# Four interleaved attention layers on one core: larger matmul pieces in crowded chunks, even pacing in the others, and another order at a layer's end

## The chip, the cores and the metric

The kernel runs on one core of one Trainium2 chip. The metric is the device time of one launch in microseconds (us); the median of three runs is used. Engines: TensorE (PE) does matmuls, ScalarE (ACT) the exponentials, VectorE (DVE) and GpSimd (POOL) the elementwise work, SyncE (SP) issues the DMAs.

## The reference

The input x has 2048 rows (positions) of 512 features. Four layers follow each other: A, B, A, B. Each adds an attention block to its input; A and B have their own weights, and both layers of a kind use the same ones.

```python
# H = 32 heads, Dh = 16, S = 2048, D = 512
qkv = layernorm(x) @ wqkv          # split into q, k, v, 32 heads of 16
scores = q @ k.T * 16 ** -0.5
# A: only 0 <= i - j < 256 is kept (a sliding window); B: all of it
p = softmax(scores)
x = x + (p @ v) @ wo
```

## The kernel before

Layers are numbered 0 to 3: 0 and 2 are the sliding ones (A), 1 and 3 the dense ones (B). Queries are taken in four chunks `c` of 512 columns. A chunk has eight groups `qd` of four heads. In a sliding layer a group has three steps (`WTILES`), so a chunk has 24 steps. In each step TensorE makes two score tiles (L722), ScalarE takes their exponential (L726), GpSimd zeroes what lies outside the window (L789, L792: five or so selects of 128x256 a step), and TensorE multiplies with the values (`PV`, L799). The PV of a step is issued two steps later (`pvq`, `flush(2)`). After a group's last PV an epilogue on VectorE (L694 to L710) divides by the sums and makes two fp16 halves of the output, `oh`.

Everything else is *side work*, laid between the steps: projections of keys `K(l, c)` and queries `Q(l, c)`, values `VV(l, c)`, the output projection with residual, statistics and normalisation `OO(l, c)`, DMA transposes of the normalised rows `T(l, c)`, preparation of weights `PR`. For layer 3, keys and queries come in quarters of the heads: `K3(c, ht)`, `Q3(c, ht)`. A projection consists of units: each unit accumulates 12 matmuls into one of two PSUM banks (an fp16 product in three terms over four blocks of 128) and is then evicted by ScalarE and VectorE. `VV` with half of the heads has matmuls 256 wide instead of 512. The names in the profile: `w`, `w_h` weights of keys and queries, `wv` of values, `wo` of the output, `xc` the transposed input, `sp` the evicted projection, `sq` its squares.

Python writes the order of TensorE's instructions once, when the kernel is built; the chip runs them in that order. A model clock (`clock`, 0.222 us a matmul) decides what is ready. In each step of a sliding layer, `Side.step` first issues transposes and preparation that are due, then side work until the amount spent reaches `due`, which grows linearly to the chunk's whole cost at step 22; at most about 3 us a step. A unit is cut into pieces of `RUN = 4` matmuls. `finish()` issues at the chunk's end what is left, with no step in between. Weights are loaded when a work is opened, and two can be open at a time (`WB = 2`). A `T` becomes due 9 us of the model clock after its `OO`, its four transposes 2.3 us apart, and is counted as done 6 us after the last.

`keys` and `queries` end with squares: a matmul (L557) of each unit's squares sums them per head; for keys VectorE takes the maximum (L573), for queries it writes a row `m` (L585, L589) that a DMA stores beside the queries. `key_shift` (L599) takes the maximum over the chunks and writes a row `mk` beside the keys `kf`; the dense layer's loads `kt<-kf` read it. Before, `mk` and `m` shared one buffer (tag `m`).

Costs that decide below: `PK = 48 * MM + 0.3` = 10.96 for K or Q, `PV = PO` = 10.66 for VV or OO, a quarter for K3, half for a VV of half the heads.

## Time and profile before

| | us |
|---|---|
| median of 3 runs | 2760.53 (2757.52 to 2761.16) |
| the profiled execution, its own time | 2759.46 |
| its span, first to last instruction | 2757.7 |
| PE busy | 2633.6 (95%) |
| ACT busy | 2385.2 (86%) |
| DVE busy | 955.0 (35%) |
| POOL busy | 566.3 (21%) |

A stage is read from its own rows, not from the shares of the whole: the dense layers run from about 509 to 1463 us and from 1787 us on, the sliding layers before each of them. In a timeline row stand the start, the duration, engine, source line, operation, output and inputs, the number of instructions merged, and in brackets how long the engine was idle before and what ended that. A row of a table by stretches has the stretch, its length, and each engine's busy time with the number of instructions, then the granted clock of TensorE, the DMA engines' share and GB/s. A row of waits has who waited for whom, the total in us, how often, and the longest.

### The profile page before, as it was taken

What the parts mean: (1) busy time and instruction counts of PE and PEld (TensorE: products, weight loads), DVE (VectorE), ACT (ScalarE), POOL (GpSimd) and SP (SyncE); (2) the same over time, 40 slices, a digit from 0 to 9 for tenths busy, and PEclk for the clock granted to TensorE, in tenths of its full rate; (3) what the DMA queues carried; (4) which work ended last, traced back from release to release, by engine and by line L of the source; (5) the groups of instructions that cost most, each with busy time, mean ns of one, the idle gap of its engine ahead of it and who ended that gap; (6) DMA issues with size and microseconds to landing.
All of it is one profiled execution on the core that took longest, in us unless ns stands there. A gap on an engine that the chain in (4) does not pass through costs nothing.

```text
span 2757.7 us, 59654 instructions
## 1 busy us (share of the span) xinstructions
PE 2633.6 (95%) x24358; PEld 776.5 (28%) x24358; DVE 955.0 (35%) x2059; ACT 2385.2 (86%) x2687; POOL 566.3 (21%) x1129
## 2 busy tenths in 40 slices
PE   8988999999999999999999989899999999999997
PEld 4333344322222222222223333522222222222221
DVE  7668756111131113211315676412222222222222
ACT  3665665799999999999996778399999999999997
POOL 2576663000000000000004688100000000000000
PEclk9999999999999999999999999999999999999999
DMA  6876766422232224222325474623334343333331
GB/s 217 230 222 209 220 212 191 141 78 72 94 92 89 71 86 111 78 68 81 109 72 161 152 202 135 179 63 103 110 112 122 120 120 105 102 110 114 98 95 56
DMA packets 317501, 344.78 MB, mean 125 GB/s; under 512 B 113056, under 2 KB 233376, under 8 KB 311200
## 3 DMA queue, kind: packets, MB, share of 16 engines
q1 hardware_dynamic: 317216, 340.86, 40.8%
q8 instruction: 193, 3.16, 0.5%
q14 instruction: 92, 0.75, 0.1%
HBM read 228.07 MB, written 96.99 MB: 118 GB/s over the span
## 4 chain that ended last, share of the span: by engine, by line
PE 74%; DVE 7%; ACT 7%; issue 6%; DMA 3%; POOL 2%; SPq 0%; ACTq 0%; DVEq 0%; POOLq 0%
PE acc L766 30%; PE s L722 19%; PE acc L434 10%; PE b L437 9%; ACT e L726 6%; PE acc L799 4%; PE bs L437 1%; DVE ot L694 1%; DVE xh L476 1%; DVE sp L535 1%; DVE xh L470 1%; DVE xn L470 1%; DMA kt<-kw 1%; POOL e L789 0%; DMA xc<-xh 0%
## 5 line engine op out<-in xcount | busy, mean ns | idle before, releaser
L726 ACT ACTIVATE e<-s 128x1024 f32<-128x1024 f32 (+2 forms) x2432 | 2244.8, 1122 | 135.0 <-PE s L722 121.7
L766 PE MATMUL acc<-e,vt 128*17 128x512 f32 x8192 | 1077.9, 598 | 5.4 <-DVE ot L694 4.5
L722 PE MATMUL s<-qt,kt 64*128 64x512 f16 (+3 forms) x5504 | 774.9, 355 | 58.6 <-ACT e L726 32.3
L722 PEld LDWEIGHTS <-kt 64*128 64x128 f16 x5504 | 202.6, 94 | 807.9 <-issue 779.3
L792 POOL TENSOR_SCALAR_AFFINE_SELECT e<-e 128x256 f32<-128x256 f32 x512 | 226.6, 450 | 118.0 <-ACT e L726 117.6
L766 PEld LDWEIGHTS acc<-e,vt 128*17 128x17 f32 x8192 | 136.2, 95 | 379.7 <-issue 347.8
L694 DVE STREAM_TRANSPOSE ot<-acc 128x512 f32<-128x512 f32 x128 | 91.4, 714 | 400.6 <-PE acc L766 317.5
L710 POOL TENSOR_TENSOR oh<-o,oh 128x512 f16<-128x512 f32 x31 | 36.0, 1161 | 885.9 <-DVE oh L709 885.9
L789 POOL TENSOR_SCALAR_AFFINE_SELECT e<-e 128x256 f32<-128x256 f32 x448 | 199.1, 451 | 69.6 <-ACT e L726 67.8
L799 PE MATMUL acc<-e,vt 128*17 128x384 f32 (+2 forms) x2816 | 199.9, 394 | 1.9 <-POOL e L789 1.0
L437 PE MATMUL b<-xc,w 128*128 128x512 f16 x672 | 164.8, 392 | 10.8 <-DVE sp L535 8.3
L540 POOL TENSOR_TENSOR sq_h<-sp_h 128x512 bf16<-128x512 f16 x27 | 28.1, 1040 | 488.5 <-DVE sp_h L534 488.5
L534 DVE TENSOR_SCALAR sp<-acc,es 128x512 f16<-128x512 f32 x28 | 20.9, 748 | 288.9 <-PE acc L434 277.2
L534 DVE TENSOR_SCALAR sp_h<-acc,es 128x512 f16<-128x512 f32 x27 | 20.3, 751 | 286.5 <-PE acc L434 277.8
L434 PE MATMUL acc<-xc,w_h 128*32 128x512 f16 x1296 | 108.6, 379 | 2.3 <-DVE km L573 2.3
L540 POOL TENSOR_TENSOR sq<-sp 128x512 bf16<-128x512 f16 x28 | 29.1, 1040 | 397.2 <-DVE sp L534 397.2
L434 PE MATMUL acc<-xc,w 128*32 128x512 f16 x1344 | 108.9, 379 | 0.3
L646 DVE COPY vt<-acc 128x256 f32<-128x256 f32 (+1 forms) x36 | 18.5, 513 | 258.2 <-PE acc L434 258.2
L681 DVE TENSOR_TENSOR dx<-acc,gcol 128x512 f32<-128x512 f32 x60 | 41.5, 692 | 176.8 <-PE acc L434 176.8
L434 PE MATMUL acc<-wo,oh 128*32 128x512 f16 x1296 | 101.3, 379 | 0.0
L437 PEld LDWEIGHTS <-w 128*128 128x128 f16 x720 | 67.0, 100 | 114.8 <-issue 49.3
L437 PE MATMUL b<-wo,oh 128*128 128x512 f16 x390 | 95.1, 384 | 2.3 <-DVE dx L660 2.1
(167 smaller groups left out, 1754.3 us busy)
## 6 DMA issues: line engine op xcount, KB each, us to landing
kt<-kf SPq DMA_DIRECT2D x128, 512.0 KB
qt<-qs SPq DMA_DIRECT2D x128, 256.0 KB
xd<-x SPq DMA_DIRECT2D x96, 256.0 KB
x<-xd SPq DMA_DIRECT2D x96, 256.0 KB
w<-wd SPq DMA_DIRECT2D x20, 1024.0 KB
kt<-kw SPq DMA_DIRECT2D x64, 256.0 KB
qs<-sp SPq DMA_DIRECT2D x48, 256.0 KB
wo<-wd SPq DMA_DIRECT2D x12, 1024.0 KB
```

The costliest lines, as they stand in the source:

```text
L434: nc.tensor.matmul(ps[g:g + 32], a[:, g:g + 32], b, start=(i == 0), stop=(i == len(pairs) - 1), skip_group_check=True)
L437: nc.tensor.matmul(ps, a, b, start=(i == 0), stop=(i == len(pairs) - 1))
L470: norm1 = lambda o: nc.vector.tensor_scalar(o, xs[i], mv[:, i, 0:1], y[:, i:i + 1], op0=ALU.subtract, op1=ALU.mult)
L540: nc.gpsimd.tensor_tensor(sq, sp[:, 0], sp[:, 0], ALU.mult)
L681: nc.vector.tensor_tensor(d, ps, gcol[1], ALU.mult)
L694: nc.vector.transpose(ot.rearrange("p b r -> p (b r)"), a)
L722: nc.tensor.matmul(ps[:, h, s0:s0 + wd_], kt[R * h:R * h + R, pr, kc:kc + P], qt[R * h:R * h + R, pr, qc:qc + wd_], start=True, stop=True)
L726: nc.scalar.activation(e[:, :, w0:w1], ps[:, :, w0:w1], AF.Exp, scale=SCALE)
L766: nc.tensor.matmul(a[32 * h:32 * h + DH + 1, :], V[l, qd // 4, j // 8][:, j % 8, 4 * (qd % 4) + h, :], es_[h // 2][:, h % 2, :], start=(j ...
L789: nc.gpsimd.affine_select(v, v, pattern=[[0, 2], [-1, P]], compare_op=ALU.is_gt, fill=0.0, base=0, channel_multiplier=1)
L792: nc.gpsimd.affine_select(v, v, pattern=[[0, 2], [1, P]], compare_op=ALU.is_ge, fill=0.0, base=0, channel_multiplier=-1)
L799: nc.tensor.matmul(a[32 * h:32 * h + DH + 1, q * P:(q + nb) * P], V[l, (4 * c + j) // 4][:, j % 4, 4 * qd + h, :], es_[h // 2][:, h % 2, s ...
```

## The change

1. A chunk of a sliding layer whose side work costs less than `FEW * MM * steps` = 7 x 0.222 x 24 = 37.3 us keeps pieces of four; the others issue whole units of 12. In chunks with pieces of four, `due` is no longer cumulative: each step takes an equal part of what is left over the steps left, less half a piece.
2. In layer 2, `VV(3, 0)` for the first half of the heads moves from the tail after the last chunk into that chunk, and `K3(2, 0)` moves from the chunk to the head of the tail.
3. After layers 0 and 2 the key shift, which first issues the waiting squares, becomes a work that is ready 1.2 us of the model clock later, so that a unit of the last values may come before it.
4. The shift's row has a buffer of its own, 128 wide instead of 512, and is stored in 16 pieces a head instead of 4.

```diff
-RUN = 4
+RUN, FEW = 4, 7
...
-        PH["unit"], PH["now"], PH["extra"] = None, None, 0
+        PH["unit"], PH["now"], PH["extra"], PH["run"] = None, None, 0, 12
...
-                elif PH["win"] and i % RUN == RUN - 1:
-                    yield RUN * us
+                elif i % PH["run"] == PH["run"] - 1:
+                    yield PH["run"] * us
...
-        m = vp.tile([P, QC], F16, name=f"mk{l}_{ht}", tag="m", bufs=1)
-        nc.vector.tensor_scalar(m[r], ones[r], kx[r], -0.515, op0=ALU.mult, op1=ALU.mult)
+        m = vp.tile([P, P], F16, name=f"mk{l}_{ht}", tag="mk", bufs=1)
+        nc.vector.tensor_scalar(m[r], ones[r, :P], kx[r], -0.515, op0=ALU.mult, op1=ALU.mult)
         for t in range(NHT) if ht is None else (ht,):
-            nc.sync.dma_start(rows(kf)[8 * t:8 * t + 8, 7, :].rearrange("h (c n) -> h c n", n=QC),
-                              m[32 * t:32 * t + 8, None, :].broadcast_to([8, NQ, QC]))
+            nc.sync.dma_start(rows(kf)[8 * t:8 * t + 8, 7, :].rearrange("h (c n) -> h c n", n=P),
+                              m[32 * t:32 * t + 8, None, :].broadcast_to([8, NT, P]))
...
             s0, due = self.spent, self.cost * self.k / (self.steps - 2)
+            if PH["run"] < 12:
+                due = s0 + (self.cost - s0) / max(self.steps - self.k, 2) - RUN / 2 * MM
             while self.q and self.spent < due and self.spent - s0 < 3:
...
+                if win:
+                    PH["run"] = RUN if sd.cost < FEW * MM * sd.steps else 12
                 ops = load(l, c, qds[0])
...
+    def shifted(l, ht):
+        key_shift(l, ht)
+        yield -1e-6
...
-        return [OO(2, 2), T(3, 2), K3(2, 0, True)]
+        return [OO(2, 2), VV(3, 0, True, (0,)), T(3, 2)]
...
-             2: [VV(3, 0, True, (0,)), OO(2, 3, True), VV(3, 1, True, (0,), late(3)), VV(3, 2, True, (0,), late(3)), Q3(0, 0, True, late(3)), T(3, 3), K3(3, 0, True)]}
+             2: [K3(2, 0, True), OO(2, 3, True), VV(3, 1, True, (0,), late(3)), VV(3, 2, True, (0,), late(3)), Q3(0, 0, True, late(3)), T(3, 3), K3(3, 0, True)]}
...
-            key_shift(l + 1, 0 if l else None)
-            all_of(lasts[l], works[l + 1][0])
+            shift = Work(later(lambda: shifted(l + 1, 0 if l else None)), 0.0)
+            shift.ready = clock[0] + 1.2
+            all_of([shift] + lasts[l], works[l + 1][0])
```

The remaining hunks replace `RUN if PH["win"] else 12` by `PH["run"]` where a unit ends, and let `shift3` call `shifted`.

More of the change, by code (lines that the diff above doesn't have):

```diff
@@ L549, in project @@
                 nc.sync.dma_start(d[:, 2], sp[:, 0])
-            yield -MM if PH["full"] else -(RUN if PH["win"] else 12) * MM
+            yield -MM if PH["full"] else -PH["run"] * MM
         return sqs
@@ L646, in values @@
                     nc.vector.tensor_copy(to, fr)
-            yield -us if PH["full"] else -(RUN if PH["win"] else 12) * us
+            yield -us if PH["full"] else -PH["run"] * us
     def wo(l, c, tail):
@@ L665, in wo @@
                 XN[l + 1, c] = norm(l + 1, c, xs, tail)
-            yield -MM if PH["full"] else -(RUN if PH["win"] else 12) * MM
+            yield -MM if PH["full"] else -PH["run"] * MM
     def wo_part(c, t):
@@ L1022, in Q3 @@
         return Work(later(queries, 3, c, act, ht), PK / 4, ("Q3", c, ht), [("T", 3, c), *after], True)
+    def shifted(l, ht):
+        key_shift(l, ht)
+        yield -1e-6
     def shift3(ht):
-        def gen():
-            key_shift(3, ht)
-            yield -1e-6
-        return Work(gen(), 0.0, None, [("K3", c, ht) for c in range(NQ)])
+        return Work(shifted(3, ht), 0.0, None, [("K3", c, ht) for c in range(NQ)])
     def O3(c, ht):
```

## The prediction

> **What bounds the kernel now.** I read the page first, then a table of the stages, then who waits for whom in the sliding layers, then TensorE's timeline at the places the change touches.
>
> ```profile
> span 2757.7 us, 59654 instructions
> ...
> PE   8988999999999999999999989899999999999997
> ```
>
> The two dense layers fill most of the span and nothing in them is edited but one buffer. TensorE's row falls below 9 in slices 1 to 8 and 20 to 26 of 69 us: the two sliding layers. I cut these into their chunks of 512 queries:
>
> ```profile
> core 0: us, PE busy (x) PEld busy (x) DVE busy (x) ACT busy (x) POOL busy (x), PEclk, DMA share, GB/s
> 65.30:142.80 77.50, 68.62 (x521) 23.72 (x521) 50.01 (x110) 47.95 (x71) 42.12 (x95) 0.93 0.83 231
> 142.80:243.10 100.30, 88.50 (x780) 35.35 (x779) 70.12 (x144) 63.28 (x78) 71.28 (x150) 0.97 0.72 221
> 243.10:357.60 114.50, 102.53 (x845) 41.21 (x844) 83.25 (x161) 70.68 (x89) 77.24 (x140) 0.94 0.75 213
> 357.60:450.90 93.30, 90.18 (x859) 39.09 (x858) 54.35 (x115) 63.19 (x78) 61.17 (x149) 1.00 0.70 216
> ...
> 1462.90:1534.30 71.40, 64.90 (x516) 22.90 (x513) 45.73 (x107) 44.51 (x64) 38.46 (x92) 0.95 0.63 199
> 1534.30:1603.70 69.40, 63.06 (x684) 24.48 (x680) 48.75 (x109) 52.36 (x58) 56.56 (x134) 1.00 0.57 165
> 1603.70:1669.60 65.90, 63.19 (x686) 24.88 (x686) 45.07 (x102) 49.55 (x55) 53.22 (x125) 1.00 0.65 183
> 1669.60:1724.00 54.40, 50.11 (x609) 19.71 (x608) 36.56 (x83) 44.28 (x48) 48.04 (x119) 1.00 0.39 118
> 1724.00:1743.80 19.80, 13.06 (x108) 7.43 (x109) 12.56 (x29) 4.16 (x7) 6.62 (x15) 0.83 0.65 153
> 1743.80:1786.80 43.00, 38.15 (x269) 25.72 (x267) 19.88 (x44) 11.48 (x25) 0.00 (x0) 1.00 0.69 193
> ```
>
> Four chunks of layer 0, four of layer 2, then layer 2's end in two rows. TensorE is the busiest engine in every row, so its instructions, which the change only reorders, are a floor; what can be won or lost is its idle time. The worst row is 1724.0 to 1743.8: 13.06 of 19.80 us busy, at 0.83 of the clock.
>
> In layer 0's four chunks TensorE waits for these, in us:
>
> ```profile
> PE s L722 <- ACT e L726: 17.5, 21, 3.6
> PE b L437 <- DVE sp L535: 8.3, 6, 3.2
> ...
> PE b L437 <- DVE dx L660: 2.1, 1, 2.1
> ```
>
> The first is scores held up because ScalarE has not emptied a score buffer; the other two are projection units held up because a bank is not yet evicted.
>
> The price of a step with and without side work, from the last chunk of layer 2:
>
> ```profile
> 1692.23 0.61 PE L722 MATMUL s<-qt,kt 64*128 64x128 f16 x8
> ...
> 1694.74 0.39 PE L722 MATMUL s<-qt,kt 64*128 64x256 f16 x4 [0.52 <-ACT e L726]
> ...
> 1697.02 0.61 PE L722 MATMUL s<-qt,kt 64*128 64x384 f16 x8
> ...
> 1698.55 1.04 PE L437 MATMUL b<-wo,oh 128*128 128x512 f16 x4
> 1699.52 0.61 PE L722 MATMUL s<-qt,kt 64*128 64x128 f16 x8
> ```
>
> A step with one piece of four runs from 1697.02 to 1699.52, 2.50 us. The bare step at 1692.23 and the step with a piece after it take 4.79 together, so an isolated bare step costs 2.29. A piece adds about 0.97, so TensorE alone would need 2.50 - 0.97 = 1.53 for a bare step: about 0.7 us is lost at each. In a row of bare steps ScalarE sets the pace: 44.28 us for 48 exponentials is 0.92 each, 1.85 a step.
>
> **Layer 2's end.** This is the largest term.
>
> ```profile
> 1724.59 2.05 PE L799 MATMUL acc<-e,vt 128*17 128x128 f32 x16 [0.60 <-DVE ot L694]
> 1732.67 4.11 PE L437 MATMUL b<-xc,w_h 128*128 128x512 f16 x12 [6.03 <-DMA xc<-xh]
> 1736.71 1.92 PE L799 MATMUL acc<-e,vt 128*17 128x256 f32 x32
> 1738.56 1.48 PE L437 MATMUL b<-wv,xc 128*128 128x256 f16 x12
> ...
> 1743.81 0.38 PE L437 MATMUL b<-wo,oh 128*128 128x512 f16 x1
> ```
>
> The key unit of chunk 2, K3(2,0), stands in order ahead of the last two PV groups and waits 6.03 us for its transposed input; the last PVs, their epilogue and the whole tail wait behind it. Then four half-width value units fill the time until O is ready, and the output projection begins at 1743.81. What releases it:
>
> ```profile
> 1711.96 0.68 DVE L660 TENSOR_TENSOR dx<-b,gcol 128x512 f32<-128x512 f32 x1
> ...
> 1730.22 0.40 POOL L792 TENSOR_SCALAR_AFFINE_SELECT e<-e 128x256 f32<-128x256 f32 x1
> ...
> 1738.70 0.72 DVE L694 STREAM_TRANSPOSE ot<-acc 128x512 f32<-128x512 f32 x1 [0.41 <-PE acc L799]
> ...
> 1741.80 0.69 DVE L710 TENSOR_TENSOR oh<-o,oh 128x512 f16<-128x512 f32 x1
> ```
>
> The epilogue after the last PV takes 1742.49 - 1738.63 = 3.9 us. GpSimd's last select ends at 1730.62, so the last PV could not have begun before that.
>
> The change puts the value units VV(3,0) into the chunk and K3(2,0) at the head of the tail. The chunk's cost becomes 10.66 + 5.33 = 15.98; by the new formula every step owes at least 15.98/24 - 0.44 > 0, so a piece is issued in each step from the fourth on: 12 output pieces in steps 4 to 15, then the 12 half-wide value pieces. The stage starts at 1669.6, three bare steps at 1.9 bring it to 1675.3, and 12 x 2.50 to 1705.3; OO(2,2) then ends some 6 us before the 1712.0 that the dx row marks, and the normalisation and its transposes (landed at 1732.67, 20.7 us after that dx) come at about 1726. The value pieces cost 1.48/3 = 0.49 a step in steps that otherwise wait for ScalarE (1.53 + 0.49 = 2.02 against 1.85): nearly nothing, and 9 steps at 2.1 to 2.2 end the scores at about 1724, as before. GpSimd has some 33 selects left at step 19 (begun about 1712) at 0.40 (48.04/119) to 0.5 us: last select 1727 to 1730; PVs done at about 1730 (1728 to 1731). K3(2,0) runs inside the 3.9 us of the epilogue. The output projection starts at about 1734 (1732 to 1737) instead of 1743.8: **-9.5 us (-7 to -12)**. The late end is K3(2,0) still waiting for its transposes. The cover that is lost, the value units, was worth 5.2 us; the epilogue is now bare for 3.9 - 2.76 = 1.1 us.
>
> On the clock: the unit behind the 6.03 us gap took 4.11 us where the same unit takes 2.76 at 1598.79 (row below). The Trainium skill, "TensorE: Matmul & The Clock Gate", Part 1, says that an idle window of about 3.4 us halves the clock; the trace agrees for this gap. By that rule the new waits, shorter and split by K3(2,0), may leave the clock whole; I take nothing for it either way.
>
> **The other chunks of layer 2, new pacing.** In pieces of four, a step now takes the rest of the cost over the rest of the steps instead of catching up.
> - Chunk 0 (cost 32.6): before, its last unit work came in blocks of 16 and left the last three steps bare. Spread out, it saves two or three bare steps at 0.7: -2 us (-4 to 0).
> - Chunk 1 (24.4): the formula gives one piece a step for 15 steps. Two units of queries come first (6 pieces, as OO(2,0) is not loaded yet), so OO(2,0) ends in step 17 instead of 14, 44 us into the stage instead of 39.
>
> ```profile
> 1572.55 1.04 PE L437 MATMUL b<-wo,oh 128*128 128x512 f16 x4
> ...
> 1598.79 2.76 PE L437 MATMUL b<-xc,w_h 128*128 128x512 f16 x12
> ...
> 1603.71 0.61 PE L722 MATMUL s<-qt,kt 64*128 64x128 f16 x8 [2.16 <-DMA kt<-kw]
> ```
>
> K3(0,0) ran 25.2 us after OO's last piece without a wait; by the 20.7 us above its input has 4 us to spare, which the 5 us use up. SyncE's queue is in order, so the loads of the next chunk stand behind these transposes too (the 2.16 us). Against it, the bare steps before K3 shrink. +1.5 us (-2 to +6).
> - Chunk 2 (24.1): OO(2,1) ends in step 13, some 6 us later, but value units and two bare steps still separate it from K3(1,0): -0.5 us (-3 to +3).
>
> **Layer 0.** Chunk 0 (35.6, under the limit of 7 x 0.222 x 24 = 37.3) gets the even pacing: no blocks of 12 that outrun the eviction, fewer bare steps at the end: -2 us (-5 to +3). Chunks 1 to 3 (47.7, 54.2, 48.9) go to whole units of 2.664 at 2.17, 2.46 and 2.22 a step, so some 4, 2 and 4 steps get none: 10 x 0.7 = +7. Against that, one unit a step gives each bank a full step to be evicted: of 8.3 + 2.1 us of bank waits I take half, -5; and fewer breaks (three pieces 3 x 0.97 against 2.70 for a unit in place, 0.2 each, about ten): -2. Sum 0 (-7 to +7). The longest bank wait, 3.2 us, I leave, because the eviction stands in VectorE's queue behind a normalisation.
>
> **The squares and the shift's buffer.**
>
> ```profile
> 497.63 0.38 PE L557 MATMUL bs<-sq,hsum 128*32 128x512 bf16 x1 [0.86 <-ACT sq L538]
> ...
> 509.14 0.61 PE L722 MATMUL s<-qt,kt 64*128 64x512 f16 x4 [0.67 <-DMA kt<-kf]
> ```
> ```profile
> 1775.72 0.38 PE L557 MATMUL b<-sq_h,hsum 128*32 128x512 bf16 x1 [1.12 <-ACT sq_h L538]
> ...
> 1779.04 0.34 DVE L606 TENSOR_SCALAR mk<-ones,kx 32x512 f16<-32x512 f16 x1 [2.05 <-DMA qs<-m]
> ...
> 1782.10 1.63 SPq L743 DMA_DIRECT2D kt<-kf  x3
> ...
> 1786.81 0.73 PE L722 MATMUL s<-qt,kt 64*128 64x512 f16 x4
> ```
>
> After layer 0 the dense layer waits for its keys, which wait for the shift, which waits for the last square at 497.63; filling TensorE before it moves idle time behind it: 0 (-1 to +1.5). After layer 2 both ends move: TensorE's work ends 1.1 us earlier, and the shift no longer waits 2.05 us for the queries' row: -1 us (-1.2 to +1.6). The shift's row is now written in pieces of 256 bytes. The Trainium skill, "DMA: Bandwidth & Descriptors", Specifications, says that writes under 512 bytes cost a read-modify-write; no run here shows it. Taking that transfer at twice the time between its issue and the keys' issue, an estimate by that page, the -1 would be about +1.6.
>
> **Sum.** -9.5 - 2 + 1.5 - 0.5 - 2 + 0 + 0 - 1 = -13.5 us. The profiled execution took 2759.46 us, so 2746; the median of the runs, 2760.53, is 1.1 above it: **2747 us**.
>
> **Rivals.**
> - *The banks were the price in layer 0.* All bank waits (10.4) vanish rather than half, and the ones of ScalarE shrink with even chunks: 10 us more, 2737. For it: 3.2 us is one wait. Against: VectorE is 0.70 to 0.73 busy there and in order.
> - *The refill only moves the wait.* K3(2,0) still waits in the tail, or VectorE's normalisation under the last selects holds GpSimd and the PVs. Then the end gives 3 to 4 us and the sum is -7: 2753, and with chunk 1 at its bad end 2758.
> - *The pacing starves the keys.* OO late in chunks 1 and 2, K3 put in order before its input has landed, in both, each with the half clock that the 4.11 us row shows: +5 + 1.4 and +6 + 1.4 more, and the 7 us of bare steps in layer 0 with nothing back: 2747 + 21 = 2768. It decides if OO(2,0) ends more than 4 us later. Against: bare steps before K3 absorb most of it.
>
> **Chances.** Forecast 0.58; banks 0.14; moved wait 0.17; starved keys 0.11. The wait of 6.03 us in front of the last PVs is the surest item. What lies under 2755 (0.2%, about what a measurement of this kernel can tell from no change) is the forecast, the banks and a little of the moved wait: faster 0.74; same 0.15; slower 0.11. The independent bounds add, root of squares, to about 8 us; reaching towards the moved wait gives 2737 to 2759.
>
> **What would show it.** Right: at layer 2's end no wait of TensorE over 4 us and OO within 10.5 us of the last score; scores of that chunk still ending near 54 us after its start; clock over 0.9 there. Chunk 0 of layer 2 without blocks of 16. Wrong: a w_h unit waiting for xc in any chunk; layer 0's chunks 1 to 3 longer than 308 us together; keys for the dense layer landing later after layer 2 than the value units end.

## The result and the profile after

| | before | after |
|---|---|---|
| median, us | 2761.18 (22 runs, 2757.52 to 2766.96) | 2757.59 (22 runs, 2752.29 to 2764.30) |
| ratio, 95% interval | | 0.9985 (0.9979 to 0.9992) |
| span of the profiled execution, us | 2757.7 | 2755.3 |

The change gains about 4 us, less than 0.2%, where 13.5 were forecast. On the page TensorE's row differs from before in one digit, a 9 for an 8 in slice 24, where layer 2's second and third chunk lie (the other slices below 9 are 1, 3, 4, 26 and 40, before and after):

```profile
span 2755.3 us, 59647 instructions
...
PE   8988999999999999999999999899999999999997
```

The same table by stretches, cut at the same events as in the prediction (first scores of each chunk, last scores, first matmul of the output projection OO(2,3), first scores of layer 3):

```profile
65.30:142.90 77.60, 68.63 (x523) 23.31 (x522) 48.24 (x110) 48.90 (x70) 43.50 (x96) 0.93 0.86 225
142.90:245.60 102.70, 88.38 (x783) 35.99 (x784) 71.35 (x144) 62.47 (x79) 71.80 (x149) 0.97 0.73 228
245.60:360.50 114.90, 103.41 (x845) 41.59 (x844) 87.09 (x161) 69.14 (x90) 75.42 (x140) 0.94 0.70 205
360.50:456.30 95.80, 90.28 (x859) 39.25 (x858) 53.27 (x115) 61.54 (x77) 61.88 (x149) 1.00 0.71 211
1465.90:1538.60 72.70, 64.58 (x514) 22.23 (x512) 45.85 (x107) 44.17 (x62) 40.88 (x95) 0.95 0.62 180
1538.60:1608.90 70.30, 65.22 (x689) 24.84 (x690) 48.19 (x108) 51.97 (x60) 56.11 (x133) 0.98 0.62 181
1608.90:1674.20 65.30, 63.37 (x689) 24.70 (x686) 43.96 (x103) 49.56 (x56) 53.20 (x125) 1.00 0.60 175
1674.20:1733.10 58.90, 55.54 (x649) 22.74 (x652) 45.22 (x96) 46.34 (x51) 53.57 (x126) 0.97 0.54 144
1733.10:1739.90 6.80, 6.73 (x70) 3.32 (x70) 4.06 (x13) 2.09 (x4) 3.16 (x8) 1.00 0.43 157
1739.90:1785.00 45.10, 38.22 (x267) 25.66 (x266) 21.48 (x47) 12.62 (x26) 0.00 (x0) 1.00 0.72 197
```

The worst row of before, 19.80 us with TensorE busy for 13.06 at 0.83 of the clock, is now 6.80 us with 6.73 busy at the full clock: 13.0 us gone. But 4.5 of them are in the row above it (54.40 before, 58.90 now), 2.1 in the row below (43.0, 45.1), 2.2 in layer 2's first two chunks, and layer 0's four chunks are 2.4 us longer in their second row and 2.5 in their last. Layer 0's end, which stands in no row, is 2.3 us shorter (58.2 us from its last row to layer 1's first scores, now 55.9).

The end of layer 2 on TensorE:

```profile
1724.16 1.06 PE L799 MATMUL acc<-e,vt 128*17 128x128 f32 x16 [1.93 <-DVE ot L694]
1725.16 1.78 PE L437 MATMUL b<-wv,xc 128*128 128x256 f16 x8
...
1729.23 1.05 PE L437 MATMUL b<-wv,xc 128*128 128x256 f16 x8
...
1737.04 2.76 PE L437 MATMUL bs<-xc,w_h 128*128 128x512 f16 x12
1739.87 2.75 PE L437 MATMUL b<-wo,oh 128*128 128x512 f16 x12
...
1785.01 0.61 PE L722 MATMUL s<-qt,kt 64*128 64x512 f16 x4 [2.66 <-DMA kt<-kf]
```

K3(2,0) at 1737.04 has no bracket: the wait of 6.03 us is gone. In the last steps there are now value pieces of eight, and the PV of the last head group but one waits 1.93 us for an epilogue. The first eight behind that wait takes 1.78 us, the next 1.05: the granted clock is at half for 3.4 us.

```profile
1725.30:1728.70 3.40, 3.40 (x28) 1.59 (x30) 3.40 (x7) 1.49 (x3) 2.57 (x6) 0.50 1.18 319
```

VectorE shows where the wait comes from:

```profile
1714.07 0.39 DVE L43 TENSOR_SCALAR v<-mv 128x4 f32<-128x4 f32 x1
...
1722.51 0.88 DVE L476 TENSOR_TENSOR xh<-xn,xh 128x512 f16<-128x512 f32 x1
1723.31 0.70 DVE L694 STREAM_TRANSPOSE ot<-acc 128x512 f32<-128x512 f32 x1
```

From 1714.07 to 1723.39 VectorE works through chunk 2's normalisation, and the reading of the accumulator (L694) comes after that in its order. Between 1739.9 and 1785.0 a new wait stands at the keys of the dense layer. SyncE's own row shows it:

```profile
1774.27 0.30 SPq L608 DMA_DIRECT2D kf<-mk  x1
1777.14 0.52 SPq L400 DMA_DIRECT2D w_h<-wd  x1
1777.76 0.61 SPq L739 DMA_DIRECT2D qt<-qs  x1
1778.46 0.93 SPq L743 DMA_DIRECT2D kt<-kf  x2
```

The shift is stored at 1774.27, five microseconds earlier than before (1779.41). Then SyncE stands 2.6 us before a load of weights, and the keys' loads stand behind it, 4.2 us after the store where it had been 2.7.

In layer 0's four chunks TensorE now waits for these:

```profile
PE s L722 <- ACT e L726: 20.6, 23, 3.6
PE b L437 <- DVE sp L535: 6.3, 4, 2.5
...
PE b L437 <- DVE dx L660: 1.6, 1, 1.6
PE b L557 <- DVE sp L535: 1.3, 1, 1.3
PE b L437 <- DVE km L573: 1.3, 2, 0.8
```

The two bank waits that the prediction counted fell by 2.5 us (forecast: 5), the waits for ScalarE grew by 3.1. But two other waits for a bank are new or longer, those for `km` (0.4 us before) and for a square's: all four together are 10.8 us before and 10.5 after.

### The profile page after: what moved, and what is told of

It reads as the page before. It is cut to its first block, busy times and chain, and to the rows that moved or that the text cites. A ratio compares the mean times of both kernels' runs of the same rounds, so it can differ in the third digit from the quotient of the medians.

```text
span 2755.3 us, 59647 instructions
## 1 busy us (share of the span) xinstructions
PE 2636.7 (96%) x24358; PEld 773.8 (28%) x24358; DVE 957.1 (35%) x2059; ACT 2380.4 (86%) x2687; POOL 571.2 (21%) x1129
## 4 chain that ended last, share of the span: by engine, by line
PE 76%; DVE 8%; ACT 7%; issue 5%; DMA 3%; POOL 1%; SPq 0%; ACTq 0%; DVEq 0%; POOLq 0%
PE acc L766 30%; PE s L722 20%; PE b L437 10%; PE acc L434 10%; ACT e L726 7%; PE acc L799 4%; PE bs L437 2%; DVE ot L694 1%; DVE xh L476 1%; DVE sp L535 1%; DVE xh L470 1%; DVE xn L470 1%; DMA x<-in_A_x_dram 0%; DMA kt<-kf 0%; DMA kt<-kw 0%
## 5 line engine op out<-in xcount | busy, mean ns | idle before, releaser
L792 POOL TENSOR_SCALAR_AFFINE_SELECT e<-e 128x256 f32<-128x256 f32 x512 | 230.0, 456 | 123.2 <-ACT e L726 122.1
L766 PEld LDWEIGHTS acc<-e,vt 128*17 128x17 f32 x8192 | 136.2, 95 | 383.4 <-issue 350.8
L694 DVE STREAM_TRANSPOSE ot<-acc 128x512 f32<-128x512 f32 x128 | 91.5, 715 | 411.2 <-PE acc L766 317.5
L789 POOL TENSOR_SCALAR_AFFINE_SELECT e<-e 128x256 f32<-128x256 f32 x448 | 201.7, 456 | 71.7 <-ACT e L726 69.3
L532 ACT ACTIVATE sp<-b,es 128x512 f16<-128x512 f32 x56 | 38.5, 687 | 79.9 <-PE b L437 76.7
L437 PEld LDWEIGHTS <-w 128*128 128x128 f16 x720 | 67.5, 100 | 121.3 <-issue 50.4
```

The lines of the kernel that those rows point to most:

```text
L437: nc.tensor.matmul(ps, a, b, start=(i == 0), stop=(i == len(pairs) - 1))
L694: nc.vector.transpose(ot.rearrange("p b r -> p (b r)"), a)
L766: nc.tensor.matmul(a[32 * h:32 * h + DH + 1, :], V[l, qd // 4, j // 8][:, j % 8, 4 * (qd % 4) + h, :], es_[h // 2][:, h % 2, :], start=(j ...
L789: nc.gpsimd.affine_select(v, v, pattern=[[0, 2], [-1, P]], compare_op=ALU.is_gt, fill=0.0, base=0, channel_multiplier=1)
L792: nc.gpsimd.affine_select(v, v, pattern=[[0, 2], [1, P]], compare_op=ALU.is_ge, fill=0.0, base=0, channel_multiplier=-1)
```

## The experiments

A stage in what follows runs from its first exponential to the first of the next (layer 0's four chunks to the last exponential of the fourth), in one profile of each kernel; its times are worked out from the traces. All runs are compared with the kernel before on the same chip; "ratio" is to before, with its 95% interval.

**Each part alone.** Four kernels, each the kernel before with one part of the change: the refill; the whole units; the even pacing; the shift's own buffer with the squares behind one unit.

```diff
# a1: refill                       # the two lists of the diff above, item 2
-        return [OO(2, 2), T(3, 2), K3(2, 0, True)]
+        return [OO(2, 2), VV(3, 0, True, (0,)), T(3, 2)]
...
# a2: whole units, old pacing
+                    PH["run"] = RUN if sd.cost < FEW * MM * sd.steps else 12
# a3: pieces of four everywhere, even pacing where the change has it
+                    PH["run"], PH["even"] = RUN, sd.cost < FEW * MM * sd.steps
# a4: items 3 and 4 of the change
+        m = vp.tile([P, P], F16, name=f"mk{l}_{ht}", tag="mk", bufs=1)
...
+            shift.ready = clock[0] + 1.2
```

> The kernel before with the value units and the key unit of layer 2's last chunk exchanged, and nothing else. Theory: the exchange is the whole gain and needs no pacing; from the first exponential of that chunk to the first of layer 3 the stage falls from 117.2 us to 108 to 110, all other stages stay within 0.5 us, and the kernel takes 7 to 9 us less than before. Rival: the chunk itself grows by the value units and by a normalisation that now lies under its last steps, as it did by 4 us in the full change; then the stage is 112 or more and the gain at most 5 us. What tells them apart: the wait for ot in the chunk's last qd and the time from its first to its last exponential (before 54.6, full change 58.9).

> The kernel before with whole units of 12 in layer 0's chunks 1 to 3 alone; old pacing everywhere. Theory: whole units lose there: chunk 1 goes from 100.2 to about 102.7 us, chunk 2 from 114.4 to 114.8, chunk 3 up to its last exponential from 89.7 to 92.1, the kernel takes 2 to 5 us more. Rival, the prediction's: bank waits halved and fewer breaks pay for the bare steps, 0 or a gain of up to 5 us, and the losses seen in the full change came down from the new pacing of chunk 0 before it.

> The kernel before with the even pacing alone in the chunks under the limit (layer 0's first, all of layer 2's), pieces of four everywhere. Theory: it gains nothing: in layer 2 chunk 0 goes from 71.7 to about 72.9 us with a wait of 6 us before K(2,3), whose weights are loaded later because the queries hold their buffer longer; chunk 1 from 69.1 to about 70.2, chunk 2 0.5 less; the kernel takes 1 to 4 us more. In the last chunk the output projection ends earlier and the key unit's wait of 6 us shrinks by 2 to 6 us, which pays some of it back. Rival, the prediction's: chunk 0 gains 2 us and the kernel is 2 to 4 us faster.

> The kernel before with the key shift behind one unit and in its own buffer alone. Theory: the shift's row is ready 2 us earlier after layer 2 but the first keys of layer 3 stand in SyncE's queue behind a weight load that waits for a buffer; from the output projection's first matmul to layer 3's first scores 43 us become 42 to 43, and layer 0's end stays within 0.5 us; in all -1 to 0. Rival: pieces of 256 bytes slow the shift's transfer, the keys land later and layer 3 begins 1 to 3 us later than before.

Measured: a1 2757.80 us, 0.9997 (0.9988 to 1.0006); a2 2760.90, 1.0004 (0.9995 to 1.0013); a3 2764.25, 1.0013 (1.0002 to 1.0023); a4 2762.43, 1.0012 (1.0002 to 1.0021); before 2760.51. None of the four gains, two cost over 3 us, and their sum, +2.6 thousandths or 7 us, has the other sign than the whole. So the parts work on each other, and the one that was to carry the forecast, the refill, pays nothing alone: last chunk and end take 116.7 us in it, 117.2 before, as a1's rival had it. a3's loss was forecast; a2 (forecast 2 to 5 us slower, rival 0 or faster) and a4 (forecast 0 to 1 us faster) fell outside their theories. The timeline of a1 says what the refill needs:

```profile
1733.03 4.74 PE L437 MATMUL bs<-xc,w_h 128*128 128x512 f16 x12 [4.60 <-issue]
1737.61 2.75 PE L437 MATMUL b<-wo,oh 128*128 128x512 f16 x12
```

K3(2,0) still waits, 4.60 us, and then runs at 4.74 us instead of 2.75. The row names no releaser; by the trace's marks of when DMAs landed, the last transpose of its input came in at 1732.94, just before. With the old pacing the value pieces went ahead in the first steps of the chunk (16 matmuls in the first alone), and OO(2,2) ended 6.8 us later, counted from the chunk's first scores, than in the next experiment (its last dx on VectorE at 1709.71, 45.6 us in; there at 1706.90, 38.8 us in). A load of the output weights (`wo`, 1 MB) was also issued ahead of the last transpose, at 1725.43 and 1726.53, and that transpose landed 6.4 us after its issue; before, with no such load in front of it, 4.2 us.

**The refill with even pacing in its own chunk.** The kernel before, the refill, and the new `due` in layer 2's last chunk only.

```diff
+            if PH.get("even"):
+                due = s0 + (self.cost - s0) / max(self.steps - self.k, 2) - RUN / 2 * MM
...
+                PH["even"] = (l, c) == (2, 3)
...   # and the two lists of a1
```

> Before, with two edits only: the refilled end of layer 2 and the even pacing in layer 2's last chunk alone. Theory (the refill pays only where the output projection's last part has finished before the scores end, and it is the even pacing of the last chunk that sees to that): the last chunk and the end together fall from 117.1 us to about 110.7 as in the whole change, the other stages stay as before, and the kernel gains 6 to 8 us, ratio 0.9972 to 0.9980. Rival (the parts add up): refill alone gave nothing and pacing alone 1.5 us in these two stages, so 1 to 2 us, ratio 0.9993 to 0.9997, and what the whole change gained beyond that comes from elsewhere.

Measured: 2749.88 us, 0.9963 (0.9951 to 0.9976), a gain of 10 us where the whole change has 4. The stretches of its last chunk, of the time to the output projection, and of the rest, and the timeline:

```profile
1668.00:1722.80 54.80, 54.21 (x651) 22.15 (x652) 38.64 (x89) 45.92 (x51) 50.75 (x122) 1.00 0.43 127
1722.80:1732.20 9.40, 8.23 (x69) 3.10 (x70) 8.65 (x21) 2.04 (x3) 5.72 (x12) 1.00 0.92 210
1732.20:1775.70 43.50, 38.13 (x270) 25.67 (x268) 21.49 (x47) 12.66 (x26) 0.00 (x0) 1.00 0.72 203
```
```profile
1729.61 2.75 PE L437 MATMUL bs<-xc,w_h 128*128 128x512 f16 x12 [0.35 <-PE acc L799]
1732.20 2.75 PE L437 MATMUL b<-wo,oh 128*128 128x512 f16 x12
```

The chunk is almost as long as before (54.40) though TensorE is busy in it for 4.1 us more (54.21, 50.11 before); K3(2,0) waits 0.35; last chunk and end fall from 117.2 to 107.6 us. The theory holds, and stage and gain go beyond it (it had about 110.7 us, and 6 to 8 us gained). The question turns round: what in the rest of the change takes 6 us away?

**Undoing one part of the whole.**

```diff
# b3: the old pacing in layer 2's chunk 0
-            if PH["run"] < 12:
+            if PH["run"] < 12 and PH["even"]:
...
+                    PH["even"] = (l, c) != (2, 0)
# b4: no whole units
-                    PH["run"] = RUN if sd.cost < FEW * MM * sd.steps else 12
+                    PH["run"], PH["even"] = RUN, sd.cost < FEW * MM * sd.steps
# d1: items 3 and 4 undone
-            all_of([shift] + lasts[l], works[l + 1][0])
+            key_shift(l + 1, 0 if l else None)
+            all_of(lasts[l], works[l + 1][0])
```

> The whole change, with the old cumulative pacing put back in layer 2's first chunk alone. Theory (even pacing there lets the keys' weights arrive late: the first chunk and the second cost 1.2 and 1.0 us more than before): these two stages go back to 71.7 and 69.2 us, and the kernel gains 1 to 3 us over the whole change, ratio to before 0.9975 to 0.9982. Rival (the order of weights is set by the works' order and not by the pace): both stages stay and the ratio stays 0.9985.

> The whole change, with pieces of four kept in every chunk and the even pacing only where the change has it: undoes the whole units in layer 0's chunks 1 to 3. Theory (whole units shorten some waits for banks and lengthen others by as much): within 1 us of the whole change, ratio to before 0.9982 to 0.9988. Rival (whole units cost what layer 0's chunks 1 and 3 were longer in the profile, 2.5 us each): the kernel gains 3 to 5 us more, ratio 0.9968 to 0.9974.

> The whole change without its fourth part: the keys' shift in its old buffer, in 512-byte pieces and ahead of the last squares. Theory (the fourth part cost 3.3 us alone and costs as much here): the kernel gains 2 to 4 us over the whole change, ratio to before 0.9970 to 0.9978. Rival (its price alone was that the end of layer 2 was late anyway; in the refilled end its buffer saves the wait of 2 us on the shift's path): the kernel loses 1 to 2 us, ratio 0.9989 to 0.9993.

Measured: b3 2758.62 us, 0.9989 (0.9980 to 0.9998); b4 2760.31, 0.9999 (0.9991 to 1.0008); d1 2757.99, 0.9993 (0.9984 to 1.0001). None of them gives the 6 us back; d1 came out as its rival had it. b3's two stages did fall (70.9 and 69.8 us, from 72.9 and 70.2), and the time did not follow. b4 is a miss on both sides: without the whole units the change is worth nothing. All three share something in the profiles: layer 0's four chunks take 387 to 389 us, as in the whole change (386.6) and in a3 (384.9), and 376 to 381 before and in a1, a2, a4 and c1. What they share and those lack is the even pacing of layer 0's first chunk.

**Adding one part to the best so far.** e1 and e2 add even pacing to c1, in layer 0's first chunk or in all of layer 2; e3 adds whole units and the shift's buffer. b1 is the whole change with the accumulators' reading put first.

```diff
# e1, on c1
-                PH["even"] = (l, c) == (2, 3)
+                PH["even"] = (l, c) in ((0, 0), (2, 3))
# e2, on c1
+                PH["even"] = l == 2
# e3: the whole change with
-            if PH["run"] < 12:
+            if PH["even"]:
...
+                PH["even"] = (l, c) == (2, 3)
# b1, on the whole change (L693)
-        with tc.high_priority(HEAD_START if l % 2 else 0):
+        with tc.high_priority(HEAD_START if l % 2 or (l, c) == (2, 3) else 0):
```

> The refill and the even pacing in layer 2's last chunk, as in c1_refill_even_last, with the even pacing in layer 0's first chunk added. Theory (even pacing there puts off work into chunks 1 and 2, whose weight preparation on ScalarE and VectorE then stands in the scores' way): layer 0's chunks 1 and 2 grow by 4 to 5 us together as in the pacing alone, and the kernel loses 3 to 5 us of c1's gain, ratio to before 0.9974 to 0.9981. Rival (layer 0 differs by chance from run to run): the ratio stays at 0.9960 to 0.9966.

> The refill and even pacing in all of layer 2, not in its last chunk alone. Theory (even pacing puts the projections of chunks 0 to 2 off by one or two steps; the last chunk then starts without free work for its first steps, its value pieces pile up in its last two, and its last reading of an accumulator waits 1.9 us behind the normalisation on VectorE): layer 2's first two chunks cost 2 us and its last 3 to 4 us more than in c1_refill_even_last, ratio to before 0.9979 to 0.9985. Rival (only the keys' weights in the first chunk are late): 2 us, ratio 0.9969 to 0.9972, with the last chunk at 54.9 us.

> The whole change with the even pacing in layer 2's last chunk alone: c1_refill_even_last with the whole units of layer 0 and the shift's own buffer behind the last squares. Theory (neither costs anything where the end is refilled, and the shift's buffer saves the wait of about 2 us that the shift's path had): ratio to before 0.9955 to 0.9965. Rival (units and shift cost what they cost alone, 1 and 3 us): 0.9974 to 0.9980.

> The whole change, with the accumulators' readings of layer 2's last chunk put ahead of the normalisation on VectorE. Theory (the last head group's values wait 1.93 us for a reading that stands behind nine microseconds of normalisation): that wait goes, the last chunk falls from 58.9 us to 56 to 57, and the kernel gains 2 to 3 us over the whole change, ratio to before 0.9974 to 0.9978. Rival (the selects on GpSimd, slower while VectorE is busy, hold these values as long): the wait is renamed, the chunk stays at 58 to 59 us and the ratio at 0.9983 to 0.9988.

Measured: e1 2757.89 us, 0.9986 (0.9978 to 0.9995); e2 2752.86, 0.9965 (0.9953 to 0.9978); e3 2750.41, 0.9960 (0.9947 to 0.9974); b1 2756.72, 0.9986 (0.9977 to 0.9994).

e1 loses 6.4 us of c1's gain by 24 steps of layer 0, more than the 3 to 5 of its theory: the interval does not touch c1's. Its second chunk is 106.1 us, 100.0 in c1, so the price is not paid in the chunk whose pace changed (77.5 and 77.4) but in the next. e3 costs nothing against c1: whole units and the shift's buffer are neutral here. In e2 the profile shows what the theory said, the first two chunks 2.8 us longer than in c1 and the last 57.7 us, but the measured ratio is c1's: a miss in the sum. b1's last chunk falls to 55.7 us as expected, the wait of 1.93 us is gone, and the time stays: 3 us of a stage that the timing does not show.

The cause in layer 0 is first looked for on ScalarE, at the turn from chunk 0 to chunk 1, in e1:

```profile
143.67 1.94 ACT L726 ACTIVATE e<-s 128x1024 f32<-128x1024 f32 x2
146.06 0.63 ACT L346 ACTIVATE w<-wr 128x512 f16<-128x512 f32 x1 [0.46 <-POOL wr L345]
147.29 0.63 ACT L346 ACTIVATE w<-wr 128x512 f16<-128x512 f32 x1 [0.60 <-POOL wr L345]
148.53 0.63 ACT L346 ACTIVATE w<-wr 128x512 f16<-128x512 f32 x1 [0.61 <-POOL wr L345]
151.91 0.63 ACT L346 ACTIVATE w<-wr 128x512 f16<-128x512 f32 x1 [2.75 <-POOL wr L345]
```

and in c1:

```profile
141.75 3.77 ACT L726 ACTIVATE e<-s 128x1024 f32<-128x1024 f32 x4
145.37 1.70 ACT L346 ACTIVATE w<-wr 128x512 f16<-128x512 f32 x3
149.30 0.63 ACT L346 ACTIVATE w<-wr 128x512 f16<-128x512 f32 x1 [2.24 <-POOL wr L345]
```

The casts of a weight preparation (L346) wait for GpSimd's products (L345), and the exponentials of chunk 1 wait behind them in ScalarE's order. In e1 no exponential runs from 145.6 to 153.0 us, in c1 from 145.5 to 150.4. The preparation of wo follows the keys K(0,1); under even pacing these get 8 matmuls a step instead of 12, and end later (their squares at 97.78 us in e1, at 93.60 in c1).

**Moving the preparation.** f4 undoes the suspect in the whole change. f1 keeps it in e1 but lets the preparation in earlier; f2 and f3 move the preparation under the old pacing.

```diff
# f4, on the whole change
-            if PH["run"] < 12:
+            if PH["even"]:
...
+                    PH["even"] = l == 2
# f1 on e1, f3 on c1: 10; f2 on c1: 18 (prep, L366)
-        yield wait(14)
+        yield wait(10 if (ty, s) == (0, 3) else 14)
```

> The whole change with the old cumulative pacing put back in layer 0's first chunk alone. Theory (of all that the change does, only this takes back the refill's gain): the kernel reaches what the refill with the last chunk's pacing reached, ratio to before 0.9960 to 0.9970, with layer 0's four chunks together 2 to 4 us shorter than in the whole change. Rival (layer 2's own pacing, 3.6 us longer there in the profiles, takes half): 0.9972 to 0.9978.

> e1_plus_l0_pace (refill, even pacing in layer 2's last chunk and in layer 0's first), with the weight preparation of layer 0's first chunk let in 4 us earlier after its load. Theory (the even pacing ends the keys' projection 3 to 4 us later, the preparation that waits for it comes as much later, and its casts then stand in ScalarE's order ahead of the exponentials of chunk 1 while GpSimd is still at the products): the casts are again one behind the other by 147 us, layer 0's second chunk falls from 106.1 us to 100 to 103, and the ratio goes from 0.9986 to 0.9968 to 0.9976. Rival (the pieces' own order in chunks 1 and 2 costs it, not the casts): second chunk 104 to 107 us, ratio 0.9983 to 0.9990.

> c1_refill_even_last (old pacing in layer 0) with the weight preparation of layer 0's first chunk let in 4 us later. Theory (the casts' place is what costs): the second chunk of layer 0 grows from 100.0 us by 3 to 6 us, as the even pacing makes it, and the ratio goes from 0.9963 to 0.9974 to 0.9985. Rival (the pieces' order costs it): within 1 us of c1, ratio 0.9960 to 0.9967.

> c1_refill_even_last with the weight preparation of layer 0's first chunk let in 4 us earlier. Theory (its last cast waits 2.24 us for GpSimd's product with the exponentials behind it): that wait goes, the second chunk of layer 0 falls by 1 to 3 us, ratio 0.9952 to 0.9960. Rival (the earlier transposes and scales disturb the first chunk as much): 0.9960 to 0.9967.

Measured: f4 2751.41 us, 0.9970 (0.9958 to 0.9982); f1 2746.62, 0.9951 (0.9939 to 0.9964), the best kernel of the study; f2 2748.57, 0.9963 (0.9951 to 0.9976); f3 2752.83, 0.9974 (0.9963 to 0.9985).

f4: with the old pacing in that one chunk the whole change gains 8 us instead of 4, layer 0's chunks 7.6 us less in the profile (379.0; forecast 2 to 4). Its interval overlaps that of the whole change by a little. f1: the casts stand elsewhere,

```profile
142.66 0.63 ACT L346 ACTIVATE w<-wr 128x512 f16<-128x512 f32 x1 [0.51 <-POOL wr L345]
143.19 3.75 ACT L726 ACTIVATE e<-s 128x1024 f32<-128x1024 f32 x4
146.81 1.69 ACT L346 ACTIVATE w<-wr 128x512 f16<-128x512 f32 x3
```

the second chunk falls from 106.1 to 97.0 us, beyond the forecast, and the time by more than the pacing had cost; the intervals of e1 and f1 do not touch. So in e1 it matters where the preparation stands. As its move wins more than the pacing had cost, it does not show that the whole cost went this way; the direct part can be read off. From the second exponential of chunk 1 to the third pass 8.4 us in all seven kernels with the even pace and the preparation in its old place, 6.0 in all nine with the old pace, and 3.5 to 3.8 in the four with the preparation earlier: the later casts cost 2.5 us there. With the preparation earlier the even pace no longer costs: layer 0's four chunks take 379.9 us in f1 and 380.4 in f3, which has the old pace, and f1 is not the slower in time.

The two others say less. f2 did not do what it was to do: its last cast came at 147.48 us, earlier than in c1, so it tests nothing. In f3 the second chunk fell to 96.4 us as the theory had it, but the first grew from 77.4 to 80.1, and its ratio lies on the wrong side of c1's, with intervals that overlap: its forecast of the time failed.

**The same in the whole change.**

```diff
# g1: the whole change; g2: the same with even pacing only in two chunks
-        yield wait(14)
+        yield wait(10 if (ty, s) == (0, 3) else 14)
...   # g2
+                    PH["even"] = (l, c) in ((0, 0), (2, 3))
```

> The whole change, with the weight preparation of layer 0's first chunk let in 4 us earlier after its load and nothing else. Theory (in the whole change as in e1 it is the preparation made late by the even pacing that costs): layer 0's second chunk falls from 102.7 us to 97 to 100, and the ratio to before goes from 0.9985 to 0.9955 to 0.9972. Rival (the whole units of chunks 1 to 3 keep the casts or their weights late): second chunk 101 to 104 us, ratio 0.9980 to 0.9988.

> The whole change with the preparation let in earlier and with even pacing only in layer 0's first and layer 2's last chunk: f1_l0_pace_prep_early with the whole units and the shift's own buffer. Theory (units and shift are worth nothing either way): as f1, ratio 0.9945 to 0.9960. Rival (units or shift cost here, 1 to 3 us): 0.9960 to 0.9968.

Measured: g1 2763.14 us, 1.0009 (1.0001 to 1.0018); g2 2761.88, 1.0004 (0.9994 to 1.0014). Both theories fall: the edit that won about 10 us in e1 loses 6 to 7 in g1, and g2, which is f1 with whole units and the shift's buffer, is some 15 us slower than f1. The first casts went where they should (141.94 to 147.8 us in g1), but layer 0's second chunk took 109.9 us. The row that did it, at that chunk's end in g1, and VectorE beside it:

```profile
247.31 2.07 PE L328 MATMUL b<-dg,onesf 128*128 128x512 f32 x2 [9.25 <-DVE dg L324]
```
```profile
237.25 0.68 DVE L470 TENSOR_SCALAR xn<-x,mv,y 128x512 f32<-128x512 f32 x1
...
246.57 0.68 DVE L324 TENSOR_TENSOR dg<-ident,wn 128x512 f32<-128x512 f32 x1
```

A later preparation has its transposed maxima ready at 236.8 us, in the midst of a normalisation on VectorE. Its scale (L324) comes after that and an epilogue, and TensorE, which has the matmul of that scale next in its order, stands for 9.25 us; in the whole change the same wait is 1.6 us, in f1 1.2. g2 has the same wait of 9.25 us, at 243.48, and a second chunk of 108.3 us. It is the same collision as at the end of layer 2, between a short step that TensorE waits for and nine microseconds of normalisation.

## Why the prediction was wrong, point by point

The profiles of the twenty kernels fall into groups by what they have in common, and the groups give each term of the sum its size. The stage times, means of the groups with the lowest and highest:

| term | without | with | measured | predicted |
|---|---|---|---|---|
| refill, with even pacing in its chunk: last chunk and end of layer 2 | 117.7 (117.2 to 118.2), 3 kernels | 108.2 (107.6 to 109.0), 7 | -9.5 | -9.5 |
| even pacing in layer 2's chunks 0 to 2: last chunk and end, refilled | 108.2 (107.6 to 109.0), 7 | 109.8 (109.2 to 111.0), 7 | +1.6 | in no term |
| the same: chunks 0 and 1 | 141.2 (140.0 to 143.4), 11 | 143.4 (142.0 to 144.5), 8 | +2.2 | -0.5 |
| the same: chunk 2 | 66.3 (65.9 to 67.5), 11 | 65.3 (65.3 to 65.4), 9 | -1.0 | -0.5 |
| even pacing in layer 0's chunk 0: layer 0's four chunks | 380.3 (376.3 to 383.4), 9 | 387.2 (384.9 to 389.1), 7 | +6.9 | -2 |
| whole units: the same, old pacing | 380.2 (376.3 to 381.4), 6 | 380.6 (379.0 to 383.4), 3 | +0.4 | 0 |
| shift's buffer: from OO(2,3) to layer 3's scores | 43.8 (43.0 to 44.5), 11 | 44.9 (43.7 to 45.5), 9 | +1.1 | -1 |

(f1, f3, g1 and g2, whose preparation comes earlier, are left out of layer 0's rows; b1, whose accumulators are read first, a1 and a3 out of those for the last chunk; b3, paced evenly in chunks 1 to 3, out of that for chunks 0 and 1.)

- **The step that failed is the pacing of layer 0's first chunk**, put at -2 us with -5 to +3. It costs 6.9 us in the profiles and 6.4 in time (e1 against c1). The step was costed inside its own chunk: bare steps saved at its end, no blocks that outrun the eviction. The blocks are gone, but TensorE's waits for banks in that chunk do not fall (1.3 us before, 1.4 after), and the chunk is no shorter. What was not followed is who waits for the work that comes later: the weight preparation behind the keys, its products on GpSimd, its casts on ScalarE ahead of chunk 1's exponentials. A slower pace puts off every work that depends on another of the same chunk, and this chain crosses three engines. Of the 6.9 us, means of the groups, 0.8 lie in chunk 0, 3.8 in chunk 1, 1.6 in chunk 2 and 0.8 in chunk 3. In chunk 1 the casts take 2.5; where the remaining 4.4 come from is not shown. Later works shift too, and gain and lose in turn: counted from the chunk's start, e1 lags c1 by 3.6 us at 160 us, leads by 1.6 at 186 us, and lags by 5.0 again from 208 us on, after a wait of 3.1 us for a square's bank.
- **Layer 2's end was right in size and, in the main, in mechanism**, though not as a term by itself. In c1 the scores end 54.7 us into the chunk (forecast 54.4), the output projection begins 64.1 us in (forecast 64.4), and K3(2,0) runs in the epilogue. The steps between were not those of the forecast, so part of this match is luck: 12 output pieces and 12 value pieces at one a step from the fourth do not fit into 24 steps; in c1 three value pieces go ahead of the output pieces, in steps that were to be bare, and two follow the last scores as an eight. The prediction took the pacing of this chunk and the refill together as one term, and they are one: without the pacing the refill gives 0.5 us (a1).
- **The clock**, for which the prediction took nothing, came back between the last scores and the output projection: 1.00 in c1 and in the whole change, 0.83 before. The Trainium skill, "TensorE: Matmul & The Clock Gate", Part 1, has the half clock follow an idle window of about 3.4 us, and the long waits agree: after 4.60 us the unit took 4.74 us (a1), after 0.35 us 2.75 (c1), and after the 9.25 us of g1 the two matmuls of a scale took 2.07. But shorter waits halved the clock too, which a rule by the length of one wait does not give: 1.93 us in the last chunk of the whole change, 2.80 us before its K3(0,0), and in e1 1.56 us before the same two matmuls, which took 2.05 (in the whole change 1.12, after 1.59 us). The half clock behind the 1.93 us cost about 1.7 us, an estimate: half of the 3.4 us that it lasted.
- **In the whole change the last chunk did not stay at 54 us**, the point that the prediction named as its sign. Even pacing in chunk 2 keeps K3(1,0) going to that chunk's last step; in the first four steps of the last chunk no value pieces come, 12 matmuls that c1 places there, and they pile up as eights in three of the last four. The rival "the refill only moves the wait" foresaw the other half, VectorE's normalisation holding the last PVs (1.93 us), and its 2753 to 2758 holds the result, but by another road: K3(2,0) does not wait, last chunk and end together fell by 6.5 us (117.2 to 110.7) where it foresaw 3 to 4, and most of what was lost again was lost in layer 0. That the time also lies in the forecast's range owes to that rival, towards which the range was drawn, and not to the sum. b1 takes the wait away and gains no time that can be measured.
- **Chunks 0 and 1 of layer 2.** The bad end of chunk 1 was on the table for the right reason (K3(0,0) waits 2.80 us now; the row names VectorE, but by the marks of landed DMAs the last transpose of its input came in 0.2 us before it began, at 1604.29), at +1 instead of +1.5. Chunk 0, put at -2, costs 1.2 in the profile of after: Q(2,2) ends later (1504.90, before 1501.88), and the next weights are loaded from SyncE's queue at 1509.27 instead of 1504.51, 2 us ahead of the last transpose of the keys' input (1511.30). That transpose landed 7.3 us after its issue, at 1518.57, where before it took 4.3 (1509.46 to 1513.80), and the projection of the keys waits 6.42 us, to 1518.81; the weights themselves had landed at 1516.53. That a slower pace also delays the loads was counted for chunk 1 and not for chunk 0. In time, e2 against c1 and e3 against f4 do not resolve layer 2's pacing: 0.2 and 1.0 thousandths, with intervals of 1.2 thousandths to either side.
- **Whole units** were right at 0 in the groups of the old pacing. With the even pacing b4 puts them at a gain of 4 us, the other way from the longer chunk 3 in the profile of after; its interval and that of after just overlap. Open.
- **The shift's buffer** frees the shift, as forecast (mk at 1774.00 instead of 1779.04, no wait), and the gain goes to the queue behind it: SyncE's next load of weights is issued at 1777.14, as a value unit ends (1777.10), and the keys stand behind that load. This was the sign listed as wrong, "keys for the dense layer landing later than the value units end". From store to the keys' issue pass 4.2 us in all nine kernels with the new buffer, 2.4 to 2.9 in the other eleven. What the pieces of 256 bytes cost is not resolved: the first keys landed 5.0 to 6.5 us after their issue with them, 4.4 to 6.0 without. Nor is the term's worth in time: a4 alone is 3.3 us slower than before, and d1, the whole change without it, 2 us slower than the whole change, with intervals that overlap.
- **Added, the terms of the groups give +2 us, not the -4 measured.** A kernel scatters by 2 to 3 us within its group, so the sum of seven is no better than that; it shows where the gain went, not its last microseconds. The measured times alone give a chain that closes: -10 us for the refill with its pacing (c1), +2 for the rest of layer 2's pacing, the whole units and the shift's buffer (f4 against c1), +4 for layer 0's pacing (after against f4); only the first is far beyond the intervals. Why moving the preparation wins in e1 and loses in g1 is shown by their rows. Which place would be good in general was not found.

## What to carry to other kernels

A list of edits is not a sum: a filler pays only if the work that it stands before is done in time, so try a refill together with the pace that it needs, and undo the rest one by one. When work is spread out more evenly, follow each work that waits for it, through every in-order engine and queue, into the next stage, and price it there. A long elementwise block on an in-order engine, here a normalisation of some nine microseconds, is the place to look at first: whatever short step falls behind it stops the busiest engine, and moving one thing by a few microseconds decides which step that is. A large load in the DMA queue is the other: transposes issued 1 to 2 us behind a load of weights landed 6.4 and 7.3 us after their issue here, 4.2 and 4.3 in the kernel before.

## What was not expected of the hardware

Spreading the side work evenly, 8 matmuls a step instead of 12, gave no shorter stage for TensorE in layer 0's first chunk (77.3 us on average over seven kernels, 76.5 over nine with the old pace), although its waits for ScalarE there fell (3.7 us before, 2.8 after; 3.5 in c1, 2.5 in e1). The granted clock fell to half after single waits as short as 1.56 and 1.93 us, where TensorE had been busy for 42 and 43% of the 3.4 us before the fall. And one and the same edit of 4 us in the order of a preparation changed the whole kernel by -10 us in one schedule (f1 against e1) and by +7 in another (g1 against after), which is as much as the largest part of the change was worth.
